# Small transposes of the logits, the route's row and the global output, from partial to full partition height

## The chip, the cores and the metric

One core of a Trainium2 chip runs the whole program in one launch. The metric is the device time in microseconds (us) of one execution. Three runs of the kernel before took 788.24, 784.57 and 785.67 us; the median, 785.67 us, is the time before.

## What is computed

The reference chains three layers over 4 batches. The first is attention of 8 heads with 64 channels: 32 global queries see all 544 keys, 512 local queries see the 32 global keys and a band of 32 positions to either side. Its output, laid out as 2176 rows (4 x 544 positions) of 512 channels, goes through an RWKV channel mix, and that through a mixture of 8 experts with a sticky route:

```
out_g = softmax(q_g k_all^T / 8) v_all            # 32 rows per head
out_l = softmax(band and global scores) v         # 512 rows per head
xk, xr = mu*x + (1-mu)*x_prev                     # x: [4, 544, 512] after the heads are joined
y = sigmoid(xr w_r) * (relu(xk w_k)^2 w_v)
logits = y w_gate                                 # 8 experts
e[s] = argmax(logits[s]) if first or gate[s] < 0.5 else e[s-1]
out[s] = softmax(logits[s])[e] * (relu(y[s] w1[e]) w2[e])
```

## The kernel before, in words

The program has two parts. Phase 1 (`phase1`) makes attention, the channel mix and the routes. Then `Experts.run` takes the rows expert by expert. Products that need full precision are made of three (`mm3`, lines 21, 23 and 24: high times high, high times low, low times high).

**Attention** runs in 16 units (a batch and a pair of heads). A unit loads, turns its keys and queries on TensorE (`prep`, L166), makes four local items (`item`: scores L207 with 64 partitions per head, softmax, turn of the weights L228, product with v L236) and one global item (`gitem`: scores L255, softmax, five turns of 64 partitions L273, product L281). At the end of `gitem` ScalarE writes the 64 x 128 output, scaled, into the tile `og` (L285), TensorE turns it with the first 64 rows and columns of the identity (L288), and VectorE copies two pieces into the mix's input (L292). That makes 16 such turns.

**The mix** (`Mix.run`) takes 17 tiles of 128 rows in nine groups (eight of two tiles, one of one). Per tile, `logits` turns y (L543), multiplies it by the gate matrix of 10 columns (psl), copies the 10 x 128 product out (`lt`, L558), turns it with a 10 x 10 piece of the identity (L562), and VectorE copies the 128 x 10 result (L565): 17 turns. Per group, `route` makes a key per row, turns each column of keys into a row on one partition (L594, whole identity), runs a maximum scan over it on VectorE (L598, tile `row`, one partition), and turns the row back, 128 keys at a time, with a 1 x 1 piece of the identity (L607), which VectorE reads (L610): 17 turns in nine places.

In a turn, the data are the operand that is loaded into the array (LDWEIGHTS) and the identity is streamed; `a*b` in the rows of the trace gives the partitions and the columns of the loaded operand.

**What sets the order.** A planner written by hand (`Sched`, with costs in us per step and priorities) decides in which order phase 1 is traced. The program is then built under `TileContext(nc,schedule_with_timeline_sim=True)`, whose scheduler orders each engine's instructions again by durations that it models; only `Experts.run` stands in a `manual_schedule()` and keeps its written order. Some steps are also chained by hand (`order`, with the lists ND and V7).

Of the kernel before, what the change touches and what calls it, by code (L numbers as in the profile page):

```python
# [10 lines left out]
F32=mybir.dt.float32; F32R=mybir.dt.float32r; BF=mybir.dt.bfloat16; I32=mybir.dt.int32  # L11
AF=mybir.ActivationFunctionType; ALU=mybir.AluOpType; X=mybir.AxisListType.X
PSUM=bass.MemoryType.PSUM; DRAM=bass.MemoryType.DRAM
P=128; D=512; F=1024; E=8; SG=32; SL=512; S=544; NB=4; T=2176; HD=64; NK=9; NCH=17
# [68 lines left out]
class Attn:  # L83


    def __init__(s,tc,ident,mask,q_l,k_l,v_l,q_g,k_g,v_g,xT,sb,ps):
        s.tc=tc; s.nc=nc=tc.nc; s.ident=ident; s.mask=mask
        s.q_l,s.k_l,s.v_l,s.q_g,s.k_g,s.v_g=q_l,k_l,v_l,q_g,k_g,v_g
        s.xT=xT; s.sb=sb; s.ps=ps
        s.gn=sb.tile([96,P],F32,name="gn",bufs=1)  # L90
        s.vn=sb.tile([P,4,2,P],F32,name="vn",bufs=1)
        s.ve=[sb.tile([P,4,2,P],F32,tag=f"v{i}",name=f"ve{i}",bufs=1) for i in range(2)]
        for t in s.ve: nc.vector.memset(t,0.0)
        s.n={}; s.pt_=[sb.tile([P,2,224],F32,name=f"pl{i}",bufs=1) for i in range(NP)]
        s.pg=sb.tile([64,608],F32,name="pg",bufs=1)
        nc.vector.memset(s.gn,0.0)
        for t in s.pt_: nc.gpsimd.memset(t,0.0)
        nc.gpsimd.memset(s.pg,0.0)
        s.V={}; s.nat=set(); s.vnat=set(); s.T={}; s.sdone={}; s.vdone={}; s.odone={}
    def places(s,t):  # L100

# [146 lines left out]
    def gitem(s,u):  # L248

        nc=s.nc; b,pr=divmod(u,4); kw,gT=s.T[u]["k"],s.T[u]["g"]  # L250
        parts=s.parts(u)
        yield op("P",.75,("s","s","g"))
        a=s.ps.tile([P,512],F32,tag="s",name="sga",bufs=2)[:64]; g=s.ps.tile([P,512],F32,tag="s",name="sgb",bufs=2)[:64,:32]
        for o,k in ((a,kw[:,:,:,32:160]),(g,gT[:,:,64:96])):
            for m,(x,y_) in enumerate(parts): nc.tensor.matmul(o,gT[:,x,:64],k[:,y_],start=m==0,stop=m==len(parts)-1)  # L255
        s.sdone[u]+=1
        p=s.pg
        mx=s.sb.tile([P,8],F32,tag="mx",name="mxg",bufs=5)[:64]
        yield op("D",1.1)
        nc.vector.reduce_max(mx[:,0:1],a,axis=X)  # L260
        nc.vector.reduce_max(mx[:,1:2],g,axis=X)
        nc.vector.tensor_reduce(out=mx[:,2:3],in_=mx[:,0:2],axis=X,op=ALU.max)
        nc.vector.tensor_scalar(out=mx[:,2:3],in0=mx[:,2:3],scalar1=-0.125,scalar2=None,op0=ALU.mult)
        yield op("A",.92,(),("s","s"))
        nc.scalar.activation(p[:,32:544],a,AF.Exp,bias=mx[:,2:3],scale=0.125,accum_out=mx[:,4:5])
        nc.scalar.activation(p[:,544:576],g,AF.Exp,bias=mx[:,2:3],scale=0.125,accum_out=mx[:,5:6])
        yield op("D",.28)
        nc.vector.scalar_tensor_tensor(out=mx[:,6:7],in0=mx[:,4:5],scalar=1e-9,in1=mx[:,5:6],op0=ALU.add,op1=ALU.add)
        nc.vector.reciprocal(mx[:,7:8],mx[:,6:7])
        yield op("P",.3,("pt","ph"),when=lambda: not s.early(u) or u in s.V)  # L270
        pt=s.ps.tile([P,512],F32,tag="pt",name="ptg",bufs=2)[:,:320]
        for c in range(5):
            nc.tensor.transpose(pt[:,c*64:(c+1)*64],s.pg[:,min(c*P,480):min(c*P,480)+P],s.ident[:64,:64])  # L273
        G=[t.rearrange("p c q -> p (c q)")[:,:320] for t in s.weights(u)]
        yield from s.split(u,EV["g"],G,pt,"pt",(.32,.4))
        yield op("P",.85,("av",),("ph",),when=lambda: u in s.V)
        o=s.ps.tile([P,512],F32,tag="av",name="avg",bufs=1)[:64,:P]
        for c in range(5):
            cs=slice(c*64,(c+1)*64)
            for m,(x,y_) in enumerate(parts):  # L280
                nc.tensor.matmul(o,G[x][:,cs],s.v(u,y_,min(c,3),c//4),start=c==m==0,stop=c==4 and m==len(parts)-1)  # L281
        s.vdone[u]+=1
        yield op("A",.16,(),("av",))
        og=s.sb.tile([64,P],F32,tag="og",name="og",bufs=1)
        nc.scalar.activation(og,o,AF.Copy,scale=mx[:,7:8])  # L285
        yield op("P",.06,("av",))
        t=s.ps.tile([P,512],F32,tag="av",name="avt",bufs=1)[:,:64]
        nc.tensor.transpose(t,og,s.ident[:64,:64])  # L288
        x=s.xT[b]
        yield op("D",.2,(),("av","g"))  # L290
        for j in range(2):
            nc.vector.tensor_copy(x[j*64:(j+1)*64,pr,1:33],t[j*64:(j+1)*64,j*32:(j+1)*32])  # L292
        yield wait(None)
        s.odone[u]+=1
# [36 lines left out]
class Mix:  # L331
# [17 lines left out]
    def consts(s,const):  # L349
        nc=s.nc  # L350
        def t(shape,name,dt=F32): return const.tile(shape,dt,name=name)
        s.i8=t([P,E],"i8"); s.i128=t([P,P],"i128"); s.i136=t([P,E*NCH],"i136"); s.tv=t([P,NCH],"tv"); s.base=t([P,NCH],"base"); s.first=t([P,NCH],"first"); s.rev=t([P,E],"rev")
        kw=dict(allow_small_or_imprecise_dtypes=True)
        nc.gpsimd.iota(s.i8,[[1,E]],base=0,channel_multiplier=0,**kw)
        nc.gpsimd.iota(s.rev,[[-1,E]],base=E,channel_multiplier=0,**kw)
        nc.gpsimd.iota(s.i128,[[1,P]],base=0,channel_multiplier=0,**kw)
        nc.gpsimd.iota(s.i136,[[1,E*NCH]],base=0,channel_multiplier=0,**kw)
        nc.gpsimd.iota(s.tv,[[P,NCH]],base=-T,channel_multiplier=1,**kw)
        nc.gpsimd.iota(s.base,[[8*P,NCH]],base=8,channel_multiplier=8,**kw)
        nc.gpsimd.memset(s.first,0.0)  # L360
        for b in range(NB):

            nc.gpsimd.affine_select(out=s.first,in_=s.first,pattern=[[P,NCH]],compare_op=ALU.not_equal,fill=1.0,base=-S*b,channel_multiplier=1)
        s.tri=t([P,P],"tri",BF); s.ones=t([P,P],"ones",BF)
        nc.gpsimd.memset(s.ones,1.0); nc.gpsimd.memset(s.tri,1.0)

        nc.gpsimd.affine_select(out=s.tri,in_=s.tri,pattern=[[1,P]],compare_op=ALU.is_gt,fill=0.0,base=0,channel_multiplier=-1)
        s.cnt=t([P,E],"cnt",BF); nc.vector.memset(s.cnt,0.0)
        w=E*NCH; s.acc=t([P,2*w],"acc"); nc.vector.memset(s.acc[:,:w],float(T)); nc.vector.memset(s.acc[:,w:],0.0); s.idx=t([P,w],"idx",I32)

        s.up=t([P,E],"up"); nc.gpsimd.memset(s.up,float(P-1)); nc.gpsimd.memset(s.up[:,0:1],-1.0)
        s.last=t([1,1],"last"); nc.vector.memset(s.last,0.0)
        s.const=t
    def load_consts(s):
        nc=s.nc; t=s.const
# [161 lines left out]
    def logits(s,g,j,t,r,N):  # L537
        nc=s.nc
        if j==0: s.Lmade[g]=0
        tag=s.ltag  # L540
        yield op("P",.44,(tag,),(),lambda: t in s.ymade)
        ps=s.rps("psy",tag).rearrange("p (d t) -> p d t",d=4)
# [8 lines left out]
        tag=s.ltag  # L551
        yield op("P",.67,(tag,),("yT",))
        ps=s.rps("psl",tag)
        for d in range(4): i=mm3(nc,ps[:10,:P],s.g[0][:,d],s.g[1][:,d],yT[0][:,d],yT[1][:,d],d==0,d==3)
        s.step(t,i)
        yield op("A",.16,(),(tag,))
        lt=s.sb.tile([10,P],F32,tag="lt",name="lt",bufs=1)
        nc.scalar.activation(lt,ps[:10,:P],AF.Copy)  # L558
        tag=s.ltag
        yield op("P",.05,(tag,))  # L560
        pl=s.rps("pslt",tag)[:,:10]
        s.step(t,nc.tensor.transpose(pl,lt,s.ident[:10,:10]))  # L562
        yield op("D",.1,(),(tag,))
        if g not in s.L: s.L[g]=s.sb.tile([P,N,10],F32,tag="L",name="L",bufs=2)
        nc.vector.tensor_copy(s.L[g][:,j],pl)  # L565
        yield wait(None)
        s.Lmade[g]+=1
    def routes(s,sched,groups):
# [6 lines left out]
    def route(s,g,tiles):  # L575
        nc=s.nc; N=len(tiles); n=N*P; t=tiles[0]; w=E*NCH; end=tiles[-1]==NCH-1
        pool=s.sb; tt=nc.vector.tensor_tensor; stt=nc.vector.scalar_tensor_tensor; ttr=nc.vector.tensor_tensor_reduce; L=s.L[g]
        sm=lambda name,w=N,dt=F32: pool.tile([P,w],dt,tag=name,name=name,bufs=2)
# [12 lines left out]
        tag=s.rtag  # L591
        yield op("P",.12*N,(tag,),when=lambda: s.scanned==g)
        ps=s.rps("psr1",tag)
        for j in range(N): i=nc.tensor.transpose(ps[0:1,j*P:(j+1)*P],fe[:,j:j+1],s.ident)  # L594
        s.step(t,i)
        yield op("D",.4+.0012*n,(),(tag,))
        row=pool.tile([1,256],F32,tag="row",name="row",bufs=1)
        nc.vector.tensor_tensor_scan(out=row[:,:n],data0=ps[0:1,:n],data1=s.tv[0:1,0:1].broadcast_to([1,n]),initial=s.last[0:1,0:1],op0=ALU.max,op1=ALU.max)  # L598
        nc.vector.tensor_copy(s.last,row[:,n-1:n])
        s.scanned=g+1  # L600
        yield op("A",.3*N)

# [1 line left out]
        tag=s.rtag  # L604
        yield op("P",.05,(tag,))
        ps=s.rps("psc",tag)
        for j in range(N): i=nc.tensor.transpose(ps[:,j:j+1],row[:,j*P:(j+1)*P],s.ident[:1,:1])  # L607
        s.step(t,i)
        yield op("D",.7,(),(tag,))
        ei=sm("ei",dt=I32); nc.vector.tensor_scalar(out=ei,in0=ps[:,:N],scalar1=-1.0,scalar2=None,op0=ALU.mult)  # L610
        nc.vector.tensor_scalar(out=ei,in0=ei,scalar1=7,scalar2=None,op0=ALU.bitwise_and)
        oh=sm8("oh",BF)
        tt(out=oh,in0=s.i8.unsqueeze(1).broadcast_to([P,N,8]),in1=ei.unsqueeze(2).broadcast_to([P,N,8]),op=ALU.is_equal)
# [436 lines left out]
```

## Time and profile before

| what | value |
|---|---|
| median of the three runs | 785.67 us |
| the profiled execution | 790.08 us |
| its span, first to last instruction | 788.3 us |
| PE busy | 737.7 us, 94% |
| DVE busy | 510.4 us, 65% |
| ACT busy | 396.3 us, 50% |
| POOL busy | 349.3 us, 44% |
| mean granted TensorE clock | 0.972 of full |

The profiled execution is 4.4 us above the median, and 1.8 us of its time lie outside the span. PE is TensorE's matmuls (turns are matmuls too), PEld its weight loads. The ends of matmuls are modelled in the trace, so a busy share does not say how well TensorE is used; the distance from one start to the next does.

### The profile page before, as it was taken

Reading aid. Unit: us, or ns where it says so; the run is one execution under the profiler, and the core shown is the slowest. Engines: PE = TensorE matmul, PEld = TensorE weight load, DVE = VectorE, ACT = ScalarE, POOL = GpSimd, SP = SyncE. Lnnn points to the kernel's source line nnn. Section 1 sums busy time; section 2 is a strip of 40 time slices with the busy share of each in tenths; the row PEclk is TensorE's granted clock in tenths of the full one; section 3 lists DMA queues with packets and bytes.
Section 4 is the critical chain, followed back from the end, with each engine's and each line's share of the span. In section 5 each row is a group of like instructions: output and inputs, shape, how many; then the busy total and the mean of one; then the engine's idle time right before and its main releaser. Section 6 shows DMA issues by size and latency. Waiting matters only on the chain. (4 is left out here: it accounts for less than half of the span.)

```text
span 788.3 us, 14122 instructions
## 1 busy us (share of the span) xinstructions
PE 737.7 (94%) x4782; PEld 621.2 (79%) x4782; DVE 510.4 (65%) x1483; ACT 396.3 (50%) x985; POOL 349.3 (44%) x473
## 2 busy tenths in 40 slices
PE   5888888999999999999999899997999999999976
PEld 3655666888888888888888788875797999988865
DVE  5698878868587695796764955665863724526351
ACT  4787565665275663655653524323761614315331
POOL 5576757743536335545442433005752422505130
PEclk9997798999999999999999999999999999999998
DMA  6584123121211211212000500216784443607130
GB/s 147 132 244 133 57 75 105 44 62 36 64 31 30 64 36 37 65 31 77 20 4 27 187 27 1 100 62 249 280 273 163 153 143 94 226 27 233 63 105 4
DMA packets 93478, 77.04 MB, mean 98 GB/s; under 512 B 70462, under 2 KB 74558, under 8 KB 93378
## 3 DMA queue, kind: packets, MB, share of 16 engines
q1 hardware_dynamic: 89618, 64.27, 27.7%
q0 software_dynamic: 3760, 11.54, 4.1%
q8 instruction: 50, 0.82, 0.4%
q14 instruction: 50, 0.41, 0.2%
HBM read 66.87 MB, written 9.70 MB: 97 GB/s over the span
## 5 line engine op out<-in xcount | busy, mean ns | idle before, releaser
L222 POOL TENSOR_SCALAR pl<-pl,mx 128x192 f32<-128x192 f32 (+1 forms) x128 | 63.1, 505 | 86.2 <-DVE mx L219 40.5
L216 ACT ACTIVATE pl<-pl,mx 128x224 f32<-128x224 f32 (+1 forms) x128 | 58.8, 461 | 35.5 <-DVE mx L213 28.4
L21 PE MATMUL psk<-xs,slot0h 128*128 128x256 f32 x256 | 74.3, 296 | 1.4 <-ACT xs L446 1.4
L23 PE MATMUL psk<-xs,slot0h 128*128 128x256 f32 x256 | 73.7, 289 | 0.0
L24 PE MATMUL psk<-xs,slot0l 128*128 128x256 f32 x256 | 73.4, 288 | 0.0
L929 POOL DMA_INDIRECT out_dram<-osb,idx x19 | 23.5, 1237 | 96.0 <-DVE osb L928 82.7
L448 POOL TENSOR_TENSOR xs<-xm,xs 128x512 fp32r<-128x512 f32 (+1 forms) x36 | 46.3, 1298 | 41.1 <-ACT xs L446 41.1
L884 ACT ACTIVATE hh<-ph 128x256 fp32r<-128x256 f32 x56 | 21.5, 384 | 84.2 <-PE ph L24 83.0
L863 POOL DMA_INDIRECT xs<-y,idx x26 | 33.9, 1305 | 63.3 <-PE pt L870 38.3
L441 POOL TENSOR_SCALAR xm<-xT,mut 128x256 f32<-128x256 f32 (+7 forms) x96 | 42.5, 457 | 36.7 <-DVE xT L292 18.0
L21 PE MATMUL psv<-slot1h,kh 128*128 128x512 f32 x136 | 55.3, 407 | 0.0
L23 PE MATMUL psv<-slot1l,kh 128*128 128x512 f32 x136 | 54.3, 400 | 0.0
L24 PE MATMUL psv<-slot1h,kl 128*128 128x512 f32 x136 | 54.2, 398 | 0.0
L228 PE MATMUL ptp<-ident,pl 128*128 128x128 f32 x256 | 44.1, 293 | 7.1 <-DVE qT L119 1.7
L21 PEld LDWEIGHTS psk<-xs,slot0h 128*128 128x128 f32 x256 | 48.6, 193 | 2.4 <-ACT xs L446 1.7
L23 PEld LDWEIGHTS psk<-xs,slot0h 128*128 128x128 f32 x256 | 49.0, 191 | 1.2
L24 PEld LDWEIGHTS psk<-xs,slot0l 128*128 128x128 f32 x256 | 49.0, 191 | 0.6
L236 PE MATMUL av<-ph,v 128*128 128x256 f32 x192 | 44.1, 290 | 2.3 <-DVE xT L292 1.8
L885 DVE SCALAR_TENSOR_TENSOR hl<-ph,hh 128x256 fp32r<-128x256 f32 x56 | 23.7, 423 | 32.9 <-ACT hh L884 32.7
L444 DVE SCALAR_TENSOR_TENSOR xm<-xT,mut,xm 128x256 f32<-128x256 f32 (+7 forms) x96 | 41.3, 463 | 3.1 <-POOL xm L441 3.0
L119 DVE TENSOR_TENSOR plo<-ptp,ph 128x512 fp32r<-128x512 f32 x48 | 32.7, 685 | 14.9 <-ACT ph L117 14.7
L228 PEld LDWEIGHTS ptp<-ident,pl 128*128 128x128 f32 x256 | 30.6, 148 | 13.9 <-issue 3.2
(730 smaller groups left out, 2462.4 us busy)
## 6 DMA issues: line engine op xcount, KB each, us to landing
st<-in_moe_w_dram SPq DMA_DIRECT2D x42, 512.0 KB, 4.5
sw<-in_moe_w_dram SPq DMA_DIRECT2D x22, 512.0 KB, 4.6
y<-r SPq DMA_DIRECT2D x17, 256.0 KB, 2.0
qn<-in_q_l_dram SPq DMA_DIRECT2D x32, 128.0 KB, 3.1
kn<-in_k_l_dram SPq DMA_DIRECT2D x32, 128.0 KB, 3.1
earlyh<-in_moe_w_k_dram SPq DMA_DIRECT2D x8, 512.0 KB, 5.0
raw<-in_moe_w_v_dram SPq DMA_DIRECT2D x8, 512.0 KB, 3.8
vn<-in_v_l_dram SPq DMA_DIRECT2D x24, 96.0 KB, 2.2
```

The lines of the kernel that those rows point to most:

```text
L21: i=nc.tensor.matmul(out,wh,xh,start=first,stop=False)
L23: nc.tensor.matmul(out,wh,xl,start=False,stop=False)
L24: return nc.tensor.matmul(out,wl,xh,start=False,stop=last)
L119: nc.vector.tensor_sub(out[1],x,out[0].bitcast(F32))
L216: nc.scalar.activation(p[:,h,ks],p[:,h,ks],AF.Exp,bias=mx[:,h:h+1],scale=-1.0,accum_out=mx[:,4+h:5+h])
L222: nc.gpsimd.tensor_scalar(out=p[:,h,ks],in0=p[:,h,ks],scalar1=mx[:,6+h:7+h],scalar2=0.0,op0=ALU.mult,op1=ALU.add)
L228: nc.tensor.transpose(pt[:,c,h],p[:,h,c*96:c*96+P],s.ident)
L236: nc.tensor.matmul(o,s.v(u,x,i,c),P_[y][:,c],start=c==m==0,stop=c==1 and m==len(parts)-1)
L441: nc.gpsimd.tensor_scalar(out=x[:,u,o:o+k],in0=s.xT[b][:,c,q:q+k],scalar1=m[:,1,c:c+1],scalar2=0.0,op0=ALU.mult,op1=ALU.add)
L444: nc.vector.scalar_tensor_tensor(out=x[:,u,o:o+k],in0=s.xT[b][:,c,1+q:1+q+k],scalar=m[:,0,c:c+1],in1=x[:,u,o:o+k],op0=ALU.mult,op1=ALU.add)
L448: nc.gpsimd.tensor_sub(xl[:,cs,:n],x[:,:,:n],xh[:,cs,:n].bitcast(F32))
L863: s.nc.gpsimd.indirect_dma_start(out=s.xs[i][:,j,:],out_offset=None,in_=s.y,in_offset=IndirectOffsetOnAxis(ap=s.idx[:,ch:ch+1],axis=0))
```

## The change

Three tiles become full height and live as long as the program part that uses them: `og` and `lt` are 128 x 128, `row` is 128 x 256. Each is set to zero once, on GpSimd, at the start. ScalarE and VectorE write the same partitions as before (64, 10 and 1), so the rest stays zero. The three turns (L288, L562, L607 of the kernel before) take the whole tile and the whole identity, so that 128 columns are streamed in place of 64, 10 or 1, and the results are 128 columns wide, of which the readers take the same 64, 10 or 1 (for the route's row, one column in 128). Line 273 names the tile otherwise and does the same as before. No planner cost and no other step is changed.

```diff
-        s.pg=sb.tile([64,608],F32,name="pg",bufs=1)
+        s.pg=sb.tile([64,608],F32,name="pg",bufs=1); s.og=sb.tile([P,P],F32,name="og",bufs=1)
...
-        nc.gpsimd.memset(s.pg,0.0)
+        nc.gpsimd.memset(s.pg,0.0); nc.gpsimd.memset(s.og,0.0)
...
-        og=s.sb.tile([64,P],F32,tag="og",name="og",bufs=1)
-        nc.scalar.activation(og,o,AF.Copy,scale=mx[:,7:8])
+        nc.scalar.activation(s.og[:64],o,AF.Copy,scale=mx[:,7:8])
         yield op("P",.06,("av",))
-        t=s.ps.tile([P,512],F32,tag="av",name="avt",bufs=1)[:,:64]
-        nc.tensor.transpose(t,og,s.ident[:64,:64])
+        t=s.ps.tile([P,512],F32,tag="av",name="avt",bufs=1)[:,:P]
+        nc.tensor.transpose(t,s.og,s.ident)
...
+        s.row=s.sb.tile([P,256],F32,name="row",bufs=1); nc.gpsimd.memset(s.row,0.0)
+        s.lt=s.sb.tile([P,P],F32,name="lt",bufs=1); nc.gpsimd.memset(s.lt,0.0)
...
-        lt=s.sb.tile([10,P],F32,tag="lt",name="lt",bufs=1)
-        nc.scalar.activation(lt,ps[:10,:P],AF.Copy)
+        nc.scalar.activation(s.lt[:10],ps[:10,:P],AF.Copy)
...
-        pl=s.rps("pslt",tag)[:,:10]
-        s.step(t,nc.tensor.transpose(pl,lt,s.ident[:10,:10]))
+        pl=s.rps("pslt",tag)[:,:P]
+        s.step(t,nc.tensor.transpose(pl,s.lt,s.ident))
...
-        nc.vector.tensor_copy(s.L[g][:,j],pl)
+        nc.vector.tensor_copy(s.L[g][:,j],pl[:,:10])
...
-        row=pool.tile([1,256],F32,tag="row",name="row",bufs=1)
+        row=s.row
...
-        for j in range(N): i=nc.tensor.transpose(ps[:,j:j+1],row[:,j*P:(j+1)*P],s.ident[:1,:1])
+        for j in range(N): i=nc.tensor.transpose(ps[:,j*P:(j+1)*P],row[:,j*P:(j+1)*P],s.ident)
...
-        ei=sm("ei",dt=I32); nc.vector.tensor_scalar(out=ei,in0=ps[:,:N],scalar1=-1.0,scalar2=None,op0=ALU.mult)
+        ei=sm("ei",dt=I32); nc.vector.tensor_scalar(out=ei,in0=ps[:,:n:P],scalar1=-1.0,scalar2=None,op0=ALU.mult)
```

## Rows read from the trace of the kernel before

**Rows 1.** The page's part 1, TensorE: busy time, share, instructions.

```profile
PE 737.7 (94%) x4782; PEld 621.2 (79%) x4782; DVE 510.4 (65%) x1483; ACT 396.3 (50%) x985; POOL 349.3 (44%) x473
```

**Rows 2.** Stages by time: length, busy us of each engine, granted clock, DMA.

```profile
0.00:160.00 160.00, 133.13 (x732) 99.24 (x733) 127.20 (x371) 104.06 (x300) 106.96 (x168) 0.90 0.45 118
160.00:430.00 270.00, 267.97 (x2017) 231.26 (x2016) 189.07 (x695) 151.79 (x446) 123.19 (x215) 1.00 0.16 40
430.00:450.00 20.00, 16.98 (x142) 15.74 (x141) 16.43 (x53) 11.56 (x25) 7.00 (x6) 0.91 0.49 168
450.00:515.00 65.00, 65.00 (x399) 54.97 (x399) 40.09 (x123) 22.89 (x44) 19.54 (x26) 1.00 0.15 53
```

**Rows 3.** Groups of PE by line and shape: the three turns, and the keys' turn.

```profile
L288 PE MATMUL avt<-ident,og 64*128 64x64 f32 x16 | 4.3, 272 | 0.7 <-ACT og L285 0.7
L562 PE MATMUL pslt<-ident,lt 10*128 10x10 f32 x17 | 3.8, 225 | 0.4 <-ACT lt L558 0.4
L594 PE MATMUL psr<-ident,fe 128*1 128x128 f32 x17 | 3.7, 286 | 1.3 <-DVE fe L588 1.3
L607 PE MATMUL psc<-ident,row 1*128 1x1 f32 x17 | 2.5, 207 | 0.0
```

**Rows 4.** Timeline of PE around a turn of lt: start, length, instruction.

```profile
177.11 0.28 PE L24 MATMUL psk<-xs,slot0l 128*128 128x256 f32 x1
177.32 0.22 PE L562 MATMUL pslt<-ident,lt 10*128 10x10 f32 x1
...
177.69 0.28 PE L23 MATMUL psk<-xs,slot0h 128*128 128x256 f32 x1
```

**Rows 5.** Timeline of PE around a lone turn of full height.

```profile
332.87 0.28 PE L24 MATMUL psk<-xs,slot0l 128*128 128x256 f32 x1
332.99 0.28 PE L236 MATMUL av<-ph,v 128*128 128x256 f32 x1
333.11 0.27 PE L228 MATMUL ptp<-ident,pl 128*128 128x128 f32 x1
...
333.34 0.28 PE L23 MATMUL psk<-xs,slot0h 128*128 128x256 f32 x1
```

**Rows 6.** Timeline of PE around a turn of og.

```profile
119.44 0.28 PE L24 MATMUL psk<-xs,slot0l 128*128 128x256 f32 x1
119.64 0.27 PE L288 MATMUL avt<-ident,og 64*128 64x64 f32 x1
...
120.07 0.28 PE L23 MATMUL psk<-xs,slot0h 128*128 128x256 f32 x1
```

**Rows 7.** Timeline of PE around the two turns of a route's row.

```profile
342.01 0.28 PE L24 MATMUL psk<-xs,slot0l 128*128 128x256 f32 x1
342.22 0.28 PE L607 MATMUL psc<-ident,row 1*128 1x1 f32 x2
...
342.65 0.28 PE L23 MATMUL psk<-xs,slot0h 128*128 128x256 f32 x1
```

**Rows 8.** Timeline of PE around the two turns of a group's keys.

```profile
182.04 0.28 PE L236 MATMUL av<-ph,v 128*128 128x256 f32 x1
182.16 0.38 PE L594 MATMUL psr<-ident,fe 128*1 128x128 f32 x2
...
182.49 0.28 PE L21 MATMUL psk<-xs,slot0h 128*128 128x256 f32 x1
```

**Rows 9.** Timeline of PE: a turn of og ahead of score products of 64 partitions.

```profile
322.58 0.28 PE L24 MATMUL psk<-xs,slot0l 128*128 128x256 f32 x1
322.78 0.27 PE L288 MATMUL avt<-ident,og 64*128 64x64 f32 x1
322.79 0.35 PE L207 MATMUL s__4453<-kw,qT 64*128 64x192 f32 x1
```

**Rows 10.** Timeline of POOL: a memset of the start, and its first idle time.

```profile
0.80 0.20 POOL masks.py:197 MEMSET ident<- 128x128 f32 x1 [0.29 <-POOLq L1037]
...
7.83 0.51 POOL L175 TENSOR_SCALAR kw<-kw 128x96 f32<-128x96 f32 x2 [0.76 <-ACT kw L111]
```

More of the change, by code (lines that the diff above doesn't have):

```diff
@@ L272, in gitem @@
         for c in range(5):
-            nc.tensor.transpose(pt[:,c*64:(c+1)*64],s.pg[:,min(c*P,480):min(c*P,480)+P],s.ident[:64,:64])
+            nc.tensor.transpose(pt[:,c*64:(c+1)*64],p[:,min(c*P,480):min(c*P,480)+P],s.ident[:64,:64])
         G=[t.rearrange("p c q -> p (c q)")[:,:320] for t in s.weights(u)]
@@ L596, in route @@
         yield op("D",.4+.0012*n,(),(tag,))
-        row=pool.tile([1,256],F32,tag="row",name="row",bufs=1)
-        nc.vector.tensor_tensor_scan(out=row[:,:n],data0=ps[0:1,:n],data1=s.tv[0:1,0:1].broadcast_to([1,n]),initial=s.last[0:1,0:1],op0=ALU.max,op1=ALU.max)
-        nc.vector.tensor_copy(s.last,row[:,n-1:n])
+        row=s.row
+        nc.vector.tensor_tensor_scan(out=row[0:1,:n],data0=ps[0:1,:n],data1=s.tv[0:1,0:1].broadcast_to([1,n]),initial=s.last[0:1,0:1],op0=ALU.max,op1=ALU.max)
+        nc.vector.tensor_copy(s.last,row[0:1,n-1:n])
         s.scanned=g+1
```

## The prediction

> **What bounds the kernel now.** I began with the page's busy times: TensorE has work 94% of the span [rows 1]. That share is an average, so I went on to the stages by time [rows 2]. From 160 to 430 us TensorE is busy 268.0 of 270 us and from 450 to 515 us all of 65, at the full clock, while the next engine, VectorE, has 189.1 of 270 (70%) and 40.1 of 65 (62%). There the start of one matmul follows from the start of the one before it, and what is taken out of TensorE's stream shortens the kernel. Before 160 us TensorE idles 26.9 us (160 less 133.1) and from 430 to 450 us another 3.0; a saving there mostly turns into a longer wait.
>
> Then I listed the turns by line and shape [rows 3]: 16 of `og` over 64 partitions, 17 of `lt` over 10, 17 of the row over 1. Their own durations (272, 225 and 207 ns) are no longer than the 286 ns of the keys' turn, which uses all 128 partitions. By durations the change would gain nothing or lose a little. What matters shows only in the timeline of PE, from start to start.
>
> **What one turn takes out of the stream.** The yardstick is the plain distance between two 256-column products, 0.12 us (332.87 to 332.99 [rows 5]); two of them are 0.235 (unrounded, 0.117 to 0.118 each).
>
> A turn of `lt`: from the product ahead of it to the second product behind it 177.69-177.11 = 0.58 us [rows 4]. Without the turn two distances would lie there, so the turn costs 0.58-0.235 = 0.345. The product before it holds the array 0.21 us in place of 0.12, and the products behind it are late too. I read this as a switch: where the number of partitions changes, on the way in and on the way out, TensorE runs empty first.
>
> A turn of full height, alone in the same kind of stream: 333.34-332.99 = 0.35, less 0.235 = 0.115 [rows 5]. Here the product ahead holds the array only 0.12. This row is the price of each of the new turns: same partitions, same loaded columns, same 128 streamed columns, same type. So a turn of `lt` saves 0.345-0.115 = 0.23 us.
>
> A turn of `og`: 120.07-119.44 = 0.63, less 0.235 = 0.395 [rows 6]; it saves 0.28.
>
> A pair of the row's turns: 342.65-342.01 = 0.64, less 0.235 = 0.405 [rows 7]. A pair of full height is the keys' turn: 182.49-182.04 = 0.45, less 0.235 = 0.215 [rows 8]. A pair saves 0.19.
>
> **How many of them count.** I went through the neighbours of all 50 turns in the timeline.
>
> `lt`: 11 of 17 stand between full-height work without an idle gap: 11 x 0.23 = 2.5 us. Of the other six two follow other turns of 64 partitions, one follows a turn of `og` (counted there), and three touch a wait. I count them at nothing; at the most they give 0.1 each, 0.6.
>
> `og`: 10 of 16 stand in a closed stream (two of them just before 160 us): 10 x 0.28 = 2.8. Five stand before 100 us or at 435 us beside waits: nothing, at most 5 x 0.28 = 1.4. One stands straight ahead of score products of 64 partitions.
>
> Row: 7 of nine places are clean: 7 x 0.19 = 1.3. One is ahead of score products, one is the last group's, in a chain of waits at the end of phase 1: nothing.
>
> The two ahead of score products lose. In the row of `og` the score product starts 0.01 us after the turn, and the 0.21 from the product ahead to them both [rows 9] is a switch that the score product needs anyway. So that turn is free now, and a full-height turn costs its 0.115: for the two places (a pair in the one) I take 0.12 and 0.12, together -0.2 with both ends 0 and -0.4.
>
> Turns: 2.5 + 2.8 + 1.3 - 0.2 = 6.4 us.
>
> The Trainium skill has a rule that speaks against the change: "TensorE: Matmul & The Clock Gate", Part 3, and its table "Why this matters for your kernels", say that matmuls of few rows in different row groups of the array run at the same time, a gain that full height gives up. The 0.01 us above agrees with it, at two of the 42 places; by the rule alone every turn would be cheap now and the sum would be a loss, and the distances of 0.58, 0.63 and 0.64 say it is not so in a stream of full-height products.
>
> **What is added.** The reader of a turn waits for its end: by the durations [rows 3] a row's turn ends some 0.08 us later (286 against 207) and one of `lt` 0.06 (286 against 225). In the closed stretches VectorE has room. In the two chains of waits (430 to 450 us, and the last group's route) one of each is on the path: 2 x 0.14 = 0.3 us lost. ScalarE and VectorE write and read as many elements as before, so I cost their edits at nothing.
>
> Three memsets on GpSimd: two of 128 columns at 0.20 us [rows 10] and one of 256 at twice that, 0.8 in all. The same rows show GpSimd idle 0.76 us before 7.83 us, waiting for ScalarE; that hides them, and I cost them at nothing. If they come behind that gap, the first scores come up to 0.8 us later. No DMA is issued, moved or passed; no wait is added, since each tile had one buffer before and its next writer waited for the same turn.
>
> **Sum.** 6.4 - 0.3 = 6.1 us, made against the profiled execution: 790.1 would become 784.0. That execution is 4.4 above the median of the runs; the saving is one of TensorE cycles in closed stretches, so I carry it over: 785.7 - 6.1 = 779.6, say 779.5 us. Bounds of the parts alone: at best 6.4+0.6+1.4+0.2 = 8.6 (777.1), at worst 6.4-0.2-0.3-0.8 = 5.1 (780.6).
>
> **Rivals.**
>
> *The freed time turns into waits.* If VectorE and ScalarE (151.8 of 270) feed the closed stretches by a chain that is just as long, TensorE only waits where it was draining. Half lost gives 782.6 us, all lost 785.7. For it: the 26.9 us of idle time before 160. Against it: 268.0 of 270 with 70% next, and only two of the counted turns lie before 160. It would also be the outcome if the turns did not leave the small mode of the array; but [rows 5, 8] show turns with the whole identity at 0.115, so the change does what it says.
>
> *Another order, slower.* The scheduler orders phase 1 by modelled durations, and the three turns grow from 64, 10 and 1 streamed columns to 128 in any model. Orders shift from the first `lt` or `og` on. In closed stretches that is harmless; in the open ones (0 to 160 and 430 to 450 us, 29.9 us of idle time [rows 2]) a product that comes one step late is paid in full. To end over 0.5% slower it must lose 6.1 + 3.9 = 10 us, a third more idle time than now. I price it at +4 to +6: 790 to 792 us. The same shift can fall well: some 4 us better, 775.5.
>
> *All turns beside 64-partition work.* By the skill's rule above: if the new order put the turns among the scores, each of the 42 places would lose 0.115, 4.8 us: 790.5. It decides once fewer than a third of the places are clean; now 28 are.
>
> **How the numbers follow.** Forecast 0.66; the waits 0.20 (half of it inside 0.5%, since 0.5% is 3.9 us); another order, slower, 0.10; turns among the scores 0.04. A measurement of this kernel tells some 0.5% from no change: the three runs lie 3.7 us apart. Faster by over 0.5% (below 781.7): the forecast's 0.66 and a little of the waits, 0.68. Within: 0.21. Slower (over 789.6): 0.11. The range must hold eight in ten: from 775.0 (bounds of the parts, and an order that falls well) to 787.0 (the waits with all lost and a little order); the likeliest case's own range is 777 to 781.
>
> **What would show it.** In the profile after, the rows of the three turns say 128*128 and 128x128 and last 270 to 290 ns; the distance from the product ahead to the second behind falls from 0.58 and 0.63 us to 0.35, and for a pair from 0.64 to 0.45. The stretch that now runs from 160 to 430 us ends some 5 us earlier against its start. If the distances shrink and the time does not, the waits are right, and a releaser of PE that hardly appears now takes the time. If the distances stay, my reading of the switch is wrong. If the turns' neighbours are others than now, the order has changed, and the idle time before 160 and from 430 to 450 us decides.

## The result, and the profile after

Six runs of the changed kernel took 793.74 to 802.37 us, median 797.58; six of the kernel before beside them had a median of 785.12. The ratio is 1.0123, interval 1.0077 to 1.0170: slower by 1.2%, where 779.5 us was predicted. The profiled execution after took 797.2 us (span 795.4) against 790.08 (788.3) before.

The page's busy times after:

```profile
PE 738.8 (93%) x4782; PEld 623.8 (78%) x4782; DVE 514.2 (65%) x1483; ACT 400.3 (50%) x985; POOL 349.0 (44%) x476
```

TensorE is 738.8 us busy against 737.7 [rows 1], with the same 4782 matmuls. The three turns in the view by line and shape:

```profile
L562 PE MATMUL pslt<-ident,lt 128*128 128x128 f32 x17 | 4.9, 289 | 0.4 <-ACT lt L558 0.4
L287 PE MATMUL avt<-ident,og 128*128 128x128 f32 x16 | 4.7, 292 | 2.5 <-ACT og L284 2.0 <-DMA ve<-in_v_l_dram 0.5
L607 PE MATMUL psc<-ident,row 128*128 128x128 f32 x17 | 3.4, 275 | 0.2 <-DVE row L598 0.2
```

They have the shapes foreseen and last 275 to 292 ns, where 270 to 290 was foreseen. PE's timeline around a turn of `og` after:

```profile
179.82 0.28 PE L23 MATMUL psk<-xs,slot0h 128*128 128x256 f32 x1
179.94 0.27 PE L287 MATMUL avt<-ident,og 128*128 128x128 f32 x1
179.97 0.36 PE L24 MATMUL psk<-xs,slot0l 128*128 128x256 f32 x1
180.17 0.28 PE L21 MATMUL psk<-xs,slot0h 128*128 128x256 f32 x1
```

From the product ahead to the second behind it is 180.17 - 179.82 = 0.35 us, where it was 0.63 [rows 6]. A pair of the row's turns (at 347.2 us) takes 0.46, where it was 0.64. So these turns became as cheap as predicted, and the kernel became slower. The stages by time after (columns as in [rows 2]):

```profile
0.00:160.00 160.00, 130.70 (x733) 96.37 (x733) 125.91 (x367) 105.03 (x297) 106.79 (x167) 0.96 0.44 118
160.00:430.00 270.00, 267.53 (x1978) 231.69 (x1979) 189.93 (x697) 153.22 (x446) 125.50 (x218) 0.99 0.16 40
430.00:450.00 20.00, 16.65 (x141) 15.38 (x140) 15.47 (x50) 10.00 (x23) 3.29 (x4) 0.91 0.32 114
450.00:515.00 65.00, 64.86 (x402) 55.64 (x402) 44.08 (x123) 23.25 (x44) 18.60 (x26) 1.00 0.15 54
```

From 160 to 430 us TensorE is as busy as before, 267.53 of 270, but gets through 1978 matmuls in place of 2017 [rows 2]. In this stage, which the prediction called closed, the loss sits inside busy time. (The page's totals alone would mislead: the span is 7.1 us longer and PE is busy only 1.1 us longer. But slow matmuls count as busy for longer, and by the clock's records the execution before spent 45 us at the lower clock, this one 33. "What stays open" sorts this.) Counting matmuls from the start, the 1200th starts 0.5 us later than before, the 2200th 6.0 us later, and the 4600th, near the end, 5.4 us later.

The order is another one as well. Compared instruction by instruction in the programs' lists (phase 1, without semaphore instructions), PE's list differs from its 39th matmul on, VectorE's from its 14th instruction, ScalarE's from its 6th: long before the first of the three turns, which is PE's 100th matmul. So the first question was whether the turns or the order cost the time.

### The profile page after: what moved, and what is told of

It is laid out like the page before. It is cut to its first block, busy times and chain, and to the rows that moved or that the text cites. A ratio compares the mean times of both kernels' runs of the same rounds, so it can differ in the third digit from the quotient of the medians.

```text
span 795.4 us, 14119 instructions
## 1 busy us (share of the span) xinstructions
PE 738.8 (93%) x4782; PEld 623.8 (78%) x4782; DVE 514.2 (65%) x1483; ACT 400.3 (50%) x985; POOL 349.0 (44%) x476
## 5 line engine op out<-in xcount | busy, mean ns | idle before, releaser
L228 PEld LDWEIGHTS ptp<-ident,pl 128*128 128x128 f32 x256 | 29.9, 145 | 14.6 <-POOL xs L449 3.4
```

Source lines behind the costliest of these rows:

```text
L228: nc.tensor.transpose(pt[:,c,h],p[:,h,c*96:c*96+P],s.ident)
```

## The experiments

Each run stands beside the kernel before on the same chip; groups of runs were made on different chips, so the ratios compare better than the medians. The third column is counted in the programs' own instruction lists: of the 48 attention items with three score products per head, how many have other products between the first head's and the second's. (The other 16, the early ones, have one score product per head.)

| run | order; turns | items with the heads apart | median us | ratio to before, interval |
|---|---|---|---|---|
| (before) | before's; small | 11 | 785.1 to 790.1 | 1 |
| (after) | the change's; whole | 22 | 797.58 | 1.0123, 1.0077 to 1.0170 |
| wide_old_order | before's; whole | 11 | 782.75 | 0.9941, 0.9909 to 0.9973 |
| small_new_order | the change's; small | 22 | 801.12 | 1.0154, 1.0119 to 1.0188 |
| tile_only | before's; small operands, whole tile | 11 | 783.80 | 0.9926, 0.9900 to 0.9953 |
| tile_all_turns | the same, with 80 turns more | 11 | 783.65 | 0.9907, 0.9876 to 0.9938 |
| memsets_only | new; small | 16 | 797.07 | 1.0116, 1.0078 to 1.0153 |
| memset_twice | new; small | 16 | 797.79 | 1.0102, 1.0071 to 1.0132 |
| memsets_on_dve | new; whole | 14 | 791.25 | 1.0018, 0.9989 to 1.0048 |
| turns_modelled | as the last; whole | 14 | 793.08 | 1.0038, 1.0010 to 1.0066 |
| og_alone | new; `og` whole | 11 | 787.44 | 0.9962, 0.9939 to 0.9985 |
| lt_alone | new; `lt` whole | 14 | 794.58 | 1.0068, 1.0042 to 1.0095 |
| row_alone | new; row whole | 14 | 797.20 | 1.0105, 1.0080 to 1.0131 |
| tile_new_order | the change's; small, whole tile | 22 | 794.98 | 1.0094, 1.0062 to 1.0126 |
| before_split | before's, 31 items split; small | 42 | 806.19 | 1.0218, 1.0188 to 1.0248 |
| change_joined | the change's, 9 items joined; whole | 13 | 791.23 | 1.0020, 0.9999 to 1.0041 |

Four more are told below.

### Turns or order?

To hold an order fixed, I edit the instruction list after the scheduler has made it. The kernel before with its tiles made persistent keeps its order exactly; then the 50 turns get whole operands and three memsets go first on GpSimd. The other way round, the change's list gets its small turns back.

```diff
+def turns(nc,rows,cols,tile):       # after the order is set
...
+    b.instructions[j]=copy.replace(i,outs=[shaped(i.outs[0],P,c)],ins=[shaped(i.ins[0],r,c),shaped(i.ins[1],r,P)],tile_size=t)
...
+    turns(nc,P,P,(P,P)); zeros(nc)      # wide_old_order: rows, streamed columns, tile
+    turns(nc,None,None,None)            # small_new_order: each turn's own small shape and tile
+    turns(nc,None,None,(P,P))           # tile_only: small operands, the whole array named as tile
```

wide_old_order. 

> The full-height turns of the change, but in the order of the kernel before: the order is set with the small turns, and the 50 turns are widened (128 partitions, 128 columns, whole array) and the three memsets put first on GpSimd afterwards, so that every engine runs the same sequence as before. If the turns save what I priced and only the new order costs (theory), 5 to 7 us faster than before, near 779. If a full-height turn itself costs more than the small one on the chip (rival 1: longer, later for its reader), as slow as the change, 795 to 800. If the three memsets at the start delay the first scores and that delay is what is lost (rival 2), about 1 us slower at most.

small_new_order. 

> The change's own order, memsets included, but the 50 turns made small again (64, 10 and 1 partitions) after the order is set. If the order is the loss and the turns are a gain (theory), slower still than the change by 5 to 7 us: 802 to 805. If the full-height turns are the loss (rival 1), back to the time before, 785.

The turns alone make the kernel faster, 0.9941; the order alone makes it slower, 1.0154. (In the change's order the turns save less than expected: small_new_order stands a little under its 802 to 805, and the step from 1.0154 to 1.0123 is 0.3%, with intervals that overlap.) In the profiles wide_old_order's 3300th matmul, at the end of phase 1, starts 5.6 us earlier than before's. The predicted price of the turns stands (6.1); what was lost came from the order: 797.58 - 782.75 = 14.8 us between two programs with the same instructions (14.4 by the ratios). The three memsets stand first on GpSimd in wide_old_order, and tile_only, which has none, is not told apart from it (0.9926 against 0.9941): on the chip they cost no time that these runs could measure.

tile_only takes the whole array as tile and leaves every operand small, with no memset. 

> The order of before and the small operands of before (64, 10 and 1 partitions and columns), but each of the 50 turns is given the whole array of 128 rows in place of a part of 32 or 64. No memset. If the cost of a small turn is the switch to another part of the array (theory), 5 to 7 us faster than before, like the full-height turns in the same order; the distance from a product over a turn to the second product falls from 0.58 to about 0.33 us. If it goes with the number of partitions or columns of the operands, no difference from before.

Its turns in the view by line and shape:

```profile
L288 PE MATMUL avt<-ident,og 64*128 64x64 f32 x16 | 3.8, 238 | 0.8 <-ACT og L285 0.7
L563 PE MATMUL pslt<-ident,lt 10*128 10x10 f32 x17 | 3.3, 195 | 0.4 <-ACT lt L559 0.4
```

In its timeline of PE a turn of `lt`:

```profile
176.63 0.28 PE L25 MATMUL psk<-xs,slot0l 128*128 128x256 f32 x1
176.75 0.18 PE L563 MATMUL pslt<-ident,lt 10*128 10x10 f32 x1
176.78 0.36 PE L22 MATMUL psk<-xs,slot0h 128*128 128x256 f32 x1
176.99 0.28 PE L24 MATMUL psk<-xs,slot0h 128*128 128x256 f32 x1
```

10 partitions and 10 columns as before, and yet 176.99 - 176.63 = 0.36 us where [rows 4] have 0.58; for the whole kernel 0.9926. So what a small turn costs is not its few partitions or columns but that its instruction names a smaller tile of the array than its neighbours (32 or 64 rows against 128). In phase 1's 3287 matmuls such changes from one to the next number 234 before and 158 in wide_old_order and tile_only. The Trainium skill, "TensorEngine Tiling (Array Packing)", Key Properties, says that changing the tiling mode drains TensorE; the two runs agree for tiles of fewer rows, with 0.23 to 0.28 us for a lone turn. For tiles of fewer columns the trace shows no such price: the products psl name 32 columns of the array, and in the kernel before one follows a product on the whole array at the plain distance, 172.90 - 172.78 = 0.12 us:

```profile
172.78 0.28 PE L24 MATMUL psk<-xs,slot0l 128*128 128x256 f32 x1
172.90 0.22 PE L21 MATMUL psl<-yT,g 128*10 128x128 f32 x1
```

tile_all_turns adds the 80 turns of the global weights (L273), 64 partitions each. 

> As tile_only (order and operands of before, whole array named in the 50 small turns), and the 80 turns of pg (16 groups of five, 64 partitions) get the whole array too. The array then changes its part 148 times in phase 1 (158 in tile_only, 234 before). If each change of part avoided is worth what tile_only showed (some 5.6 us for 76, 0.07 each): 0.7 us faster than tile_only, not to be told apart from it. If the turns of 64 partitions next to full-height products are dear as such: 3 us faster.

0.9907 is the best median of this group, but its interval overlaps tile_only's: not told apart.

### What draws the new order?

memsets_only has the persistent tiles and the three memsets, with small turns. 

> The change's tiles and its three memsets, with the small turns of before, built as usual: the scheduler then gives a third order. Theory (any edit that moves the modelled times draws a new order, and the time goes with the order): anywhere between 780 and 802, with no turn changed. Rival 1 (the turns): 785, like before. Rival 2 (the memsets at the start): like the change, 797.

It loses nearly all that the change loses. That is also where its rival 2, the memsets' own delay, put it; but wide_old_order has the same memsets first on GpSimd and is faster than before. memset_twice takes it to the extreme: the kernel before with a single memset that it already had, written a second time.

```diff
-        nc.gpsimd.memset(s.pg,0.0)
+        nc.gpsimd.memset(s.pg,0.0); nc.gpsimd.memset(s.pg,0.0)
```

> The kernel before with one line more: the memset of pg on GpSimd at the start is made twice. No turn, tile or reader is changed. As built, TensorE and ScalarE get exactly the order of the run memsets_only (TensorE's array changes its part 248 times in phase 1, against 234 before). If the order is the cause (theory): as slow as memsets_only, 795 to 799. If the tiles, their memsets or the turns matter in themselves: 785 to 789, like before, since 0.6 us of a memset that nothing waits for adds at most that.

1.0102, and its order on PE and ScalarE is that of memsets_only to the instruction. The memset itself is 0.59 us on an engine that is 44% busy. The list comes out otherwise from the first items on; that it does so because the times shift that the scheduler models is argued, not shown.

Two runs take this away: memsets_on_dve puts the memsets on VectorE, turns_modelled leaves them out of the scheduler's sight and puts them in afterwards.

> The change with its three memsets on VectorE in place of GpSimd, and nothing else different. As built, TensorE follows the order of before up to about the 160th us and another from there, and its array changes its part 162 times in phase 1 (182 in the change, 158 with the order of before and full-height turns). Theory (GpSimd's memsets at the start shift the modelled times early and draw the bad order; the turns themselves gain): 780 to 786, faster than before. If full-height turns cost as soon as the scheduler knows of them, whatever the memsets: 795 to 799.

> The change, scheduled without its memsets, which are put first on GpSimd after the order is set. TensorE's and ScalarE's order is that of memsets_on_dve. If the order decides and a memset's place does not: the same as memsets_on_dve within 2 us. If three memsets ahead of all else on GpSimd cost by themselves: later by their 0.8 us, no more.

memsets_on_dve missed its expectation of 780 to 786 us; turns_modelled came within 2 us of it, as expected. They have one and the same order on PE and ScalarE, equal to before's until about 160 us, and end at 1.0018 and 1.0038, not at the 0.994 of wide_old_order. So the wider turns, too, redraw the order once the scheduler sees them, and that gave back what they save.

### One kind of turn at a time

In each of the three only one kind is whole (its memset on VectorE), and all is scheduled anew. tile_new_order has the change's order, with small operands and the whole tile in 130 turns.

> Only the 16 turns of the global output are whole (tile of 128 x 128, memset on VectorE); the logits' and the row's turns stay small; the scheduler orders everything anew. Theory A (the new order costs, the turns gain): the turns by themselves save some 2.5 us, the redrawn order may add 0 to 10 us anywhere behind the first of these turns, so 782 to 795, and the three single parts need not add up to the three together (+0.2% with the memsets on VectorE). Theory B (one kind of turn costs by itself): the kind that costs stands at 792 or more, the other two below before, and the three differences add up to the +0.2% of the three together.

> Only the 17 turns of the logits are whole (memset on VectorE). Theory A: the turns save some 2 us, the redrawn order adds 0 to 10: 782 to 795, no additivity. Theory B: either at 792 or more or clearly below before, and the three differences add up.

> Only the 17 turns of the route's row are whole (memset on VectorE). Theory A: the turns save 1.2 us, the redrawn order adds 0 to 10: 783 to 796, no additivity. Theory B: as for the others; with the smallest saving it would be nearest to before.

> The change's own order, but the 50 turns have their small operands again and only name the whole array as their tile, and so do the 80 turns of 64 partitions of the global weights. Theory A (order sets the loss, the change of array part is the price of a turn): as the change or 1 to 3 us better, 794 to 797, and some 4 us better than the change's order with small turns in small tiles (801.1). If the operands' size mattered beside the tile: 1 us or more away from that, towards 801.

The three single effects are -0.38%, +0.68% and +1.05%; their sum, +1.35%, is not the +0.2 to +0.4% of all three (memsets_on_dve and turns_modelled). The row's turns save least and came out worst (1.2 us above the upper end that I gave). That fits draws of an order, not costs of a turn. tile_new_order is 0.6% better than small_new_order, as the price of the tile wants it.

### Which trait of the order costs?

A clue is in the timelines of the score products (L207). The two heads of an item use two halves of the array (tiles of 64 rows at rows 0 and 64). Before, an item at 142.93 us:

```profile
142.72 0.28 PE L236 MATMUL av<-ph,v 128*128 128x256 f32 x1
142.93 0.37 PE L207 MATMUL s__1688<-kw,qT 64*128 64x224 f32 x1
142.94 0.37 PE L207 MATMUL s__1689<-kw,qT 64*128 64x224 f32 x1
143.14 0.27 PE L207 MATMUL s__1688<-kw,qT 64*128 64x224 f32 x1
143.15 0.27 PE L207 MATMUL s__1689<-kw,qT 64*128 64x224 f32 x1
143.24 0.27 PE L207 MATMUL s__1688<-kw,qT 64*128 64x224 f32 x1
143.26 0.27 PE L207 MATMUL s__1689<-kw,qT 64*128 64x224 f32 x1
143.46 0.65 PE L228 MATMUL ptp<-ident,pl 128*128 128x128 f32 x4
```

The heads start 0.01 us apart and run side by side: six products in 143.46 - 142.93 = 0.53 us. After, the same item (its products are named 1689 and 1690 there) has eight other matmuls between its heads:

```profile
148.59 0.59 PE L207 MATMUL s__1689<-kw,qT 64*128 64x224 f32 x3
...
150.85 0.59 PE L207 MATMUL s__1690<-kw,qT 64*128 64x224 f32 x3
```

An item of this kind with its neighbours, from the profile after (item 1989, which stands apart in the kernel before too):

```profile
173.47 0.28 PE L21 MATMUL psk<-xs,slot0h 128*128 128x256 f32 x1
173.68 0.57 PE L207 MATMUL s__1989<-kw,qT 64*128 64x192 f32 x3
174.18 0.39 PE L23 MATMUL psk<-xs,slot0h 128*128 128x256 f32 x1
174.41 0.28 PE L24 MATMUL psk<-xs,slot0l 128*128 128x256 f32 x1
174.62 0.57 PE L207 MATMUL s__1990<-kw,qT 64*128 64x192 f32 x3
175.13 0.38 PE L21 MATMUL psk<-xs,slot0h 128*128 128x256 f32 x1
175.35 0.28 PE L23 MATMUL psk<-xs,slot0h 128*128 128x256 f32 x1
```

The heads are apart, each half of the array works alone, and the array changes its part four times in place of two. By the prediction's way of counting, one head takes 174.41 - 173.47 - 0.235 = 0.705 us out of the stream, the other 175.35 - 174.41 - 0.235 = 0.705, together 1.41. Of 352 recorded score products 228 start within 0.04 us of another before, 166 after; and of the 48 items 11 are apart before, 22 after.

The first attempt at a test failed. Within each unbroken run of score products I put the heads by turns, or one head after the other, in three orders (change_alternate, before_alternate and tile_alternate by turns; before_apart the other way):

```diff
+            new+=items[x]+items[y] if apart else [i for p in zip(items[x],items[y]) for i in p]
```

> The change's order; only within an unbroken run of score products the two heads of an item come by turns (91 pairs side by side in place of 68, of 160). Theory P (lost pairs are part of the loss): a product of 224 columns takes 0.10 us behind another of its kind, and a pair takes that once, so 23 pairs save some 2.3 us (1.5 to 4): 793.5 to 796 against 797.6. Rival (pairs do not matter, only clock and changes of part do): as the change, within 1 us.

> The kernel before, nothing else changed, but within an unbroken run one head's products come first and then the other's (48 pairs in place of 86). Theory P: 38 lost pairs at 0.10 us and up to 0.17 cost 3.8 to 6.5 us: +0.5% to +0.8%. Rival: within 0.15% of before.

> The kernel before, within an unbroken run the two heads by turns (122 pairs in place of 86). Theory P: 36 more pairs save 2 to 4 us, -0.25% to -0.5%. Rival: within 0.15% of before.

> Before's order, 130 turns with small operands in the whole array as tile, and the heads by turns (122 pairs). Theory P: 2 to 4 us better than the same without the turns of the heads, so about 0.986 to 0.988 of before. Rival: 0.99 to 0.992 as without.

1.0134 (1.0095 to 1.0174), 1.0023 (0.9992 to 1.0055), 1.0019 (0.9986 to 1.0052) and 0.9903 (0.9873 to 0.9933, median 780.71): none moved clear of its interval from the same order without the edit. By the expectations the theory would have fallen, but the edit had not done what it was for: 234 products still start beside another in before_apart, 230 in before_alternate, 180 in change_alternate. The six above are in the program one head after the other already. So inside an unbroken run the order of the heads does not matter; what can matter is only whether other products stand between the heads. The next two edits change just that, at the list made by the scheduler: before_split moves the second head's three products behind the next product of full height, in 31 items; change_joined moves the first head's three down to the second's, in 9 (the first of the products that they pass takes over their waits too).

```diff
+        if split and not gap:
...
+            I[min(k):e+1]=x+[I[e]]+y; n+=1
+        if not split and gap and all(quiet(i) and not out(i).startswith("s_") for i in gap) and k[2]<k[3]:
...
+            I[min(k):max(k)+1]=[g]+gap[1:]+x+y; n+=1
```

> The order of before, but in 31 items of three score products a head the second head's three come behind the next product of full height in place of ahead of it. Theory S (an item whose heads stand apart costs a half microsecond: three products alone take 0.52 us in the trace, the six of two heads side by side 0.53): 31 x 0.5 = 15 us, about +1.9% (10 to 18 us, part of it lost in waits). Rival C (only the changes of array part count, 54 more at some 0.1 us): 5 us, +0.7%. Rival N (neither): within 1 us.

> The change's order, but in 9 items the first head's three score products are moved down to the second's, past up to nine products of full height. Theory S: 9 x 0.5 = 4.5 us less, 793 (3 to 5 us less). Rival C (14 changes of part fewer): 1.5 us less, 796. Rival N: as the change, within 1 us.

before_split is 2.2% slower than before: 806.19 - 789.43 = 16.8 us, 0.54 for each of 31 items, where rival C (changes of part alone) said 5. One of them in its timeline (one line is added at the kernel's top, so L207 is L208 here):

```profile
144.08 0.59 PE L208 MATMUL s__1688<-kw,qT 64*128 64x224 f32 x3
144.60 0.33 PE L229 MATMUL ptp<-ident,pl 128*128 128x128 f32 x1
144.86 0.59 PE L208 MATMUL s__1689<-kw,qT 64*128 64x224 f32 x3
145.38 0.55 PE L229 MATMUL ptp<-ident,pl 128*128 128x128 f32 x3
```

The same item that took 0.53 us takes 0.52 twice. change_joined gives back most of the change's loss, 1.0020 against 1.0123, with all the rest of its order as it was. (The loss itself is repeated by change_alternate, measured beside another chip's kernel before: 1.0134.) Of the nine items seven stand together in the kernel before, two apart there too; so the run shows what an item apart costs, and not only what the change added. Item 1989 in its timeline, the one shown above of the change:

```profile
174.91 0.28 PE L25 MATMUL psk<-xs,slot0l 128*128 128x256 f32 x1
175.12 0.35 PE L208 MATMUL s__1989<-kw,qT 64*128 64x192 f32 x1
175.13 0.35 PE L208 MATMUL s__1990<-kw,qT 64*128 64x192 f32 x1
175.32 0.27 PE L208 MATMUL s__1989<-kw,qT 64*128 64x192 f32 x1
175.33 0.27 PE L208 MATMUL s__1990<-kw,qT 64*128 64x192 f32 x1
175.43 0.27 PE L208 MATMUL s__1989<-kw,qT 64*128 64x192 f32 x1
175.44 0.27 PE L208 MATMUL s__1990<-kw,qT 64*128 64x192 f32 x1
175.64 0.39 PE L22 MATMUL psk<-xs,slot0h 128*128 128x256 f32 x1
175.86 0.28 PE L24 MATMUL psk<-xs,slot0h 128*128 128x256 f32 x1
```

175.86 - 174.91 - 0.235 = 0.715 us in place of 1.41: 0.70 saved, and 9 x 0.70 = 6.3; the medians say 797.58 - 791.23 = 6.4, the ratios 1.03%, 8.1 us, and with their intervals 6.3 is not told apart from the expected 4.5. That it comes so near is in part luck. (The profiled execution of change_joined has a span of 793.0 us, only 2.4 under the change's: it stands at the upper end of its runs, 787.60 to 794.77, and spent 44 us at the lower clock, the change's 33.) The expectation left out the changes of part that go with a split.

### What stays open

The change has 11 items apart more than the kernel before. At 0.54 to 0.70 us they make 5.9 to 7.7 of the 14.8 us that its order costs. The traces tell where the rest lies, by an estimate: TensorE's busy time, counted half where it ran at the lower clock (the start, up to the clock's first record, is taken as low).

| profiled execution | span us | busy at full clock | lost at the lower clock | idle |
|---|---|---|---|---|
| before | 788.3 | 713.4 | 24.3 | 50.7 |
| before_split | 804.5 | 730.0 | 25.0 | 49.4 |
| wide_old_order | 782.8 | 705.6 | 28.4 | 48.8 |
| after | 795.4 | 716.0 | 22.8 | 56.6 |
| change_joined | 793.0 | 710.4 | 27.4 | 55.3 |
| memsets_only | 797.8 | 718.1 | 29.5 | 50.2 |

Against wide_old_order, with the same instructions, the change has 10.4 us more of busy time and 7.8 more of idle time, and lost 5.6 less at the lower clock. Splitting adds 16.6 us of busy time and joining takes 5.6 off, with the idle time 1.3 us less in both. So items apart cost busy time, some 6 to 8 of the 10.4; the remaining busy time and the 7.8 us of idle time are not explained.

The clock's part can be seen in memsets_only, in the view of stretches (PE alone, then the granted clock, the DMA share and GB/s):

```profile
135.00:140.00 5.00, 4.14 (x22) 0.50 0.18 72
140.00:145.00 5.00, 5.00 (x16) 0.50 0.00 2
145.00:150.00 5.00, 5.00 (x19) 0.79 0.00 0
```

In the kernel before:

```profile
135.00:140.00 5.00, 5.00 (x15) 0.55 0.09 15
140.00:145.00 5.00, 5.00 (x43) 1.00 0.24 92
145.00:150.00 5.00, 5.00 (x31) 1.00 0.00 0
```

In both TensorE is at 1.2 GHz (granted 0.5) after a thin stretch around 130 us. Before, it is at the full 2.4 GHz from 139.5 us on; in memsets_only only from 147.1, while it is busy with products of 512 columns that start every 0.43 us in place of 0.23. That is 13.7 us at the lower clock against 6.8, some 3.4 us lost, of the 5.2 that memsets_only loses more at the lower clock in the table. Its five items more apart make 2.7 to 3.5 us, of 4.7 more of busy time. turns_modelled is at 0.80 from 320 to 330 us and 0.69 from 330 to 340, where wide_old_order has 1.00 in both. But these are readings: no run moved a thin stretch by itself. row_alone, at 1.0105 with 14 items apart, is not explained by the count. Nor was it tried why the scheduler sets the heads apart, and no kernel was run with the heads kept together in the scheduler's own rules.

The best medians are tile_alternate's 780.71 us (0.9903) and tile_all_turns' 783.65 (0.9907): before's order kept, and the whole array named as tile in 130 turns. Both beat the kernel before and the change.

## Why the prediction was wrong

**The price of a turn: right.** 0.63 became 0.35 us, and the turns in before's order gave 0.59% (0.27 to 0.91), 4.7 us of 789, and 5.6 us at the end of phase 1 in the profiles, where the sum had 6.1. The reading of it was half right: TensorE does run empty around a small turn, but because of the tile that the instruction names; "the number of partitions" was not the cause, and tile_only gets the gain without touching a row.

**The memsets at nothing: right on the chip, wrong for the program.** Beside GpSimd's idle time [rows 10] they cost no time that the runs could tell, and they alone bring +1.16%, by the order that comes out. The step asked what the instructions do to the engines and not what they do to the list.

**"In closed stretches that is harmless": the step that failed.** The rival "another order, slower" had the right cause and 0.10 of the chance. Its price came from idle time alone (a third more than the 29.9 us of the open stages), and that price seemed unlikely. The order cost 14.8 us. It does cost idle time (7.8 us more in the change's profile than in wide_old_order's), but the larger part, 10.4 us, is busy time: TensorE stays busy and does less, and some 6 to 8 us of that are items whose heads are apart and leave half the array unused. Nor did the order shift only "from the first `lt` or `og` on": it is another one from PE's 39th matmul. The bound of an unknown order, some 4 us better to 6 worse, was too narrow. The rows for a wider one were in the trace of before: the item at 142.93 us has its heads together, and 11 items have them apart.

**The rival with the 64-partition work** came close and looked at the wrong instructions. It took from the Trainium skill, "TensorE: Matmul & The Clock Gate", Part 3, that matmuls in different row groups run at the same time, and applied it to the turns. The rule holds here, for the score products (0.01 us between the heads' starts), and a new order can undo that gain.

**The waits** had 0.20 and did not decide: in before's order the freed time came through, 0.9941.

**The range**, 775.0 to 787.0, was built from the parts' bounds and a little order; the orders that the scheduler drew in these runs end between 0.9962 (og_alone, its turns' saving included) and 1.0154 (small_new_order).

## What to carry to other kernels

Where a scheduler orders the program by modelled durations, every instruction added or widened redraws the list, and the draw can be worth more than the change: compare the lists first, and measure a change once with the order held fixed. Where two half-height products fill the array together, count how many stand unseparated; a closed stretch with a busy engine can still lose time by that. And before making operands whole, see whether naming the whole array as tile is enough.

## What was not expected of the hardware

Three products of one half of the array followed in the program by three of the other half ran by turns, each pair 0.01 us apart (142.93 and 142.94, 143.14 and 143.15). The Trainium skill, "TensorE: Matmul & The Clock Gate", Part 3, says that matmuls start strictly in program order; across two halves of the array this trace shows otherwise, and before_apart and before_alternate, equal within their intervals, agree with the trace. And a turn of 10 rows and 10 streamed columns that names the whole array takes as much out of the stream (0.36 us by the distance) as one of 128 by 128 (0.35 [rows 5]), though its own duration is 195 ns, against 289 for the whole turn of `lt` in the change.
